# First feed-forward layer in two half-precision parts, with scales found on the chip, more planned time for the scales' round trips, and two more exponential buffers

## The chip, the cores and the metric

The kernel runs on one core of a Trainium2 chip. A core has five engines with a queue each: TensorE (PE in the profile; its weight loads are the row PEld) multiplies matrices into PSUM; VectorE (DVE), ScalarE (ACT) and GpSimd (POOL) do elementwise work; SyncE (SP) here only starts DMA transfers. Each engine takes its instructions in the order in which the program gives them and waits on semaphores for the others. The metric is the device time of one execution in microseconds (us). Three executions of the kernel before took 1029.51, 1033.57 and 1035.02 us, so the median is 1033.57 us.

## The reference

A hash-masked attention over 4 batches of 8 heads, 768 positions of 64 elements, followed by a feed-forward layer ("MoE" by its name, with one expert) over 3072 tokens of 512 elements and a hidden size of 2048:

```python
mask = q_bucket[:, :, :, None] == k_bucket[:, :, None, :]   # 6 sign bits of q @ proj, k @ proj
scores = np.where(mask, scale * np.matmul(q, k.transpose(0, 1, 3, 2)), -1000000000.0)
attn = np.exp(scores - np.max(scores, axis=-1, keepdims=True))
attn = attn / (np.sum(attn, axis=-1, keepdims=True) + 1e-09)
x = np.matmul(attn, v)            # then (batch, head, seq, dim) -> (batch*seq, head*dim)
h = x @ w_in                      # 512 -> 2048
r = np.maximum(h, 0.0)
out = (s * (r * r) + b) @ w_out   # 2048 -> 512
```

The inputs q, k, v and proj are float32. The two weight matrices arrive as float64 and are read as pairs of 32-bit words.

## The kernel before, in words

**Attention.** A visit is one (batch, head); there are 32, in order, and a visit has three slots of 256 queries, so 96 slots. A slot handles two tiles of 128 queries by 768 keys. For each tile PE makes the scores in two halves (lines 519 and 520), DVE takes the row maximum (line 524), ACT the exponential with its row sum (525), DVE four small operations for the inverse (531 to 534), and POOL normalizes (543). The exponentials live in a ring of buffers `eb`: `NE` = 3 of them, plus two that are laid over the buffer `pb` in the first eight visits.

The first eight visits (batch 0; `late(w)` is false) multiply in float32: PE transposes the tile (570), ACT or DVE copies it out of PSUM (the helper's line 199), and PE multiplies it with the values (577). From visit 8 on (`late`), the tile is split into two half-precision parts by ACT and DVE (547, 548), transposed by a DMA (549), and multiplied with values that were split in the same way (584). For that the values of a batch are scaled by a power of two that the chip finds. `value_scale` loads the eight heads' values one after another into `vm` (484), takes the largest absolute value of each (485, DVE), writes the 128 row maxima to DRAM (489), reads them back spread over all partitions (490), and DVE makes the scale out of them (494 to 499). Lines 489 and 490 are the *round trip*: both are issued by SP, and 490 waits until the write of 489 is done. It is made for batches 1, 2 and 3.

**Preparing a visit.** Transposes of q and k (384), their split in two parts (386, 387), the hash product (401 to 403), its mask bits (405) and several SP transfers that stack the operands (`ks`, `aq`, `bq`, all issued by the helper on line 175). A visit is prepared while the visit before it runs.

**Handing over to the feed-forward layer.** After its second head, a pair of heads' result (`xpb`, lines 603 and 604) is split into a high and a low part in fp32r, a rounded 32-bit format (`xsb`; ACT or POOL copy on 199, POOL subtraction on 609). SP writes the parts to DRAM (`xd`) and reads them back as `xc` (631).

**Weights.** 32 blocks of 128 by 512 float64 words are fetched on ACT's queue (338) and decoded to float32 by two ACT (340, 341), two DVE (342, 343) and one POOL instruction (344). A copy and a POOL subtraction (347) make the two fp32r parts. The order is four blocks of `w_in`, four of `w_out`, and so on.

**Feed-forward.** A chunk is 256 tokens; there are 12. A chunk has eight units of two blocks of 128 hidden elements. A unit multiplies in three passes per block of 128 (high weight by high input, low weight by high input, high weight by low input: lines 645, 646, 647; 24 matmuls of 256 columns), then takes the rectifier (651), the square (652), scale and bias (653, 654), the low part (655), and multiplies with `w_out` in three passes (666 to 668; 12 matmuls of 512 columns). The whole kernel has 2304 matmuls of the first kind.

**What sets the order.** Nothing runs as written. `Plan` collects every step with its engine, an estimated duration, what it reads and writes, a priority `pr` and a `lag` (time until its result is there). `order()` plays these on a model clock: whichever engine is free takes the ready step of the lowest priority number. A step may name several engines (`any`, `some`, `copy`), and goes to the one that is done first. The resulting order is each engine's program. Attention goes ahead of the units, which have priority numbers from 1e5 on and so fill what PE has left. The first units can run once slot 21 has been handed over.

Of the kernel before, what the change touches and what calls it, by code (L numbers as in the profile page):

```python
# [10 lines left out]
F32 = mybir.dt.float32  # L11
# [128 lines left out]
def lsh_attention_moe(ctx: ExitStack, tc, q, k, v, proj, w_in, w_out, s, b, out):  # L140
# [3 lines left out]
    P = 128  # L144
# [71 lines left out]
    vsc = tile_("vsc", [P, B, 2])  # L216
    VB = [tile_(f"vb{x}", [P, NT, 4, D], F16) for x in range(2)]
# [27 lines left out]
    xsb = tile_("xsb", [P, 2, CH], F32R)  # L245
# [67 lines left out]
    dec, wt = [], {}  # L313
# [7 lines left out]
    def decode(u, pr):  # L321
        src, key = dec[u]
        box = {}

        def new():
            box["t"] = wk.tile([P, 512, 2], I32, tag=f"w{u}", name=f"raw{u}")

        def swap():
            wt[key] = wk.tile([P, 2, 512], F32R, tag=f"w{u}", name=f"w{u}")
# [3 lines left out]
        rk, wk_ = [("raw", u)], [key + (0,), key + (1,)]  # L333
# [6 lines left out]
        act(512, lambda: nc.scalar.activation(g, raw()[:, :, 1].bitcast(F32), AF.Copy, scale=float(2.0**-112)), rk + [("pace", u % PACE)], [gk], pr)  # L340
        act(512, lambda: nc.scalar.activation(raw()[:, :, 0], raw()[:, :, 0].bitcast(U32), AF.Copy, scale=float(2.0**-29)), rk, rk, pr)
        dve(256, lambda: nc.vector.tensor_scalar(raw()[:, :, 1], gi, -2**31, None, ALU.bitwise_and), [gk], rk, pr, 0.54)
        dve(512, lambda: nc.vector.scalar_tensor_tensor(gi, gi, 3, raw()[:, :, 1], ALU.logical_shift_left, ALU.bitwise_or), rk, [gk], pr, 0.88)
        pool(512, lambda: nc.gpsimd.tensor_tensor(gi, gi, raw()[:, :, 0], ALU.add), rk, [gk], pr)
        plan.add(None, 0.0, swap, [], rk + wk_, pr)
        copy(512, lambda: wt[key][:, 0], lambda: g, [gk], [key + (0,)], pr, (ACT, POOL))
        pool(512, lambda: nc.gpsimd.tensor_tensor(wt[key][:, 1], g, f32(wt[key][:, 0]), ALU.subtract), [gk, key + (0,)], [key + (1,)], pr)  # L347
# [131 lines left out]
    def value_scale(bb, pr):  # L479


        for h in range(H):
            vd = v[bb, h].rearrange("(p t) d -> p t d", t=NT)
            plan.add(SP, 0.7, lambda vd=vd: nc.sync.dma_start(vm.rearrange("p (t d) -> p t d", t=NT), vd), [], ["vm"], pr, 196608 / RATE_DMA)
            dve(1, lambda h=h: nc.vector.tensor_reduce(vmx[:, h:h + 1], vm, AX.X, ALU.max, apply_absolute_value=True), ["vm"], [("vx", h)], pr, 0.5)
        m = vmx[:, H:H + 1]
        dve(1, lambda: nc.vector.tensor_reduce(m, vmx[:, 0:H], AX.X, ALU.max), [("vx", h) for h in range(H)], ["vx"], pr, 0.16)
        dm = tc.dram_tile([P], F32, name=f"vmax{bb}")
        plan.add(SP, 0.7, lambda: nc.sync.dma_start(dm.rearrange("(p o) -> p o", o=1), m), ["vx"], [("dm", bb)], pr, 0.3)
        plan.add(SP, 0.7, lambda: nc.sync.dma_start(vm[:, 0:P], dm.rearrange("(o x) -> o x", o=1).broadcast_to([P, P])), [("dm", bb)], ["vm"], pr, 0.3)  # L490
        up, down = vsc[:, bb, 0:1], vsc[:, bb, 1:2]

        def power():
# [3 lines left out]
            nc.vector.tensor_scalar(up.bitcast(I32), down.bitcast(I32), -1, 254 << 23, ALU.mult, ALU.add)  # L497
            nc.vector.tensor_scalar(up, up, float(2.0**14), None, ALU.mult)
            nc.vector.tensor_scalar(down, down, float(2.0**-14) * STEP / TOP, None, ALU.mult)
        dve(1, power, ["vm"], ["vx", ("sc", bb)], pr, 1.1)  # L500
# [54 lines left out]
    def values(i, pr, pieces):  # L555
# [45 lines left out]
        sa, sd = (vsc[0:D, bb, 1:2], vsc[D:P, bb, 1:2]) if late(w) else (1.0, 1.0)  # L601
        sk = [("sc", bb)] if late(w) else []
        some(CH, lambda e: e.activation(xh, av[0:D], AF.Copy, scale=sa) if e is nc.scalar else e.tensor_scalar(xh, av[0:D], sa, None, ALU.mult), [("b", 4)] + sk, xk, pr, (ACT, DVE))
        dve(CH, lambda: nc.vector.scalar_tensor_tensor(xh, av[D:P], sd, xh, ALU.mult, ALU.add), [("b", 4)] + sk, xk, pr, 0.42)
        if hh:

            xk = [tk + (0,), tk + (1,)]
            copy(CH, lambda: xsb[:, 0, :], lambda: t, xk, [("xs", 0)], pr, (ACT, POOL))
# [120 lines left out]
RATE = 6.0  # L729
PACE = 2  # L730
DSTART = 3
NNAT = 1
TOP = 2.0**27
STEP = 2.0**12
TWO = 2
# [39 lines left out]
```

## Time and profile before

| | us |
|---|---|
| median of three executions | 1033.57 |
| the profiled execution's own time | 1031.19 |
| its span, first to last instruction | 1029.4 |
| PE busy | 957.0 |
| DVE busy | 643.6 |
| ACT busy | 638.2 |
| POOL busy | 604.5 |

The profile is of one execution. Its own time is 2.4 us below the median, and 1.8 us lie outside the span. A row of a group of instructions gives line, engine, operation, operands, count, busy time and mean duration. A matmul's duration runs from its start to the end of its pipeline, and the next one starts before that end. So what a matmul costs PE is the distance between two starts, which the timeline shows.

### The profile page before, as it was taken

The page shows a single profiled execution, that of the slowest core. Times are in us where ns is not written, and L with a number is a line of the kernel's source. Part 1 is how long each engine was busy: PE and PEld are TensorE (multiplying, and loading weights), DVE is VectorE, ACT ScalarE, POOL GpSimd, SP SyncE. Part 2 cuts the span into 40 slices and gives each one's busy share as a digit, 9 for nine tenths or more (in the row PEclk, how much of TensorE's full clock was granted, in tenths as well). Part 3 has the DMA queues.
Part 4 walks back from the last instruction along what each step waited for, and adds up shares of the span by engine and source line. Part 5 has one row for each costly group of instructions (what it writes and reads, how often), then busy time and mean ns, then how long its engine had stood idle before and what let it go on. Part 6 is the DMA issues. An engine that isn't in the chain of part 4 may idle for free.

```text
span 1029.4 us, 17335 instructions
## 1 busy us (share of the span) xinstructions
PE 957.0 (93%) x6072; PEld 818.4 (80%) x6072; DVE 643.6 (63%) x1207; ACT 638.2 (62%) x1128; POOL 604.5 (59%) x559
## 2 busy tenths in 40 slices
PE   7977787698799999999999999999999999999998
PEld 5655555387678898888888998888888788999986
DVE  6786986688776667778877777777877661000000
ACT  2576777577666667767777667667776674334342
POOL 1356876599786657556656575756566555333333
PEclk6896999899899999999999999999999999999999
DMA  3276766587798798899899798899898773101000
GB/s 79 78 178 177 215 169 152 145 228 192 123 215 159 158 218 184 176 211 179 180 217 195 153 226 163 171 203 177 154 231 165 150 166 73 62 1 62 22 21 21
DMA packets 318791, 155.61 MB, mean 151 GB/s; under 512 B 283040, under 2 KB 291104, under 8 KB 318704
## 3 DMA queue, kind: packets, MB, share of 16 engines
q1 hardware_dynamic: 313504, 137.46, 62.2%
q10 hardware_dynamic: 5200, 17.05, 6.4%
q8 instruction: 48, 0.79, 0.3%
q14 instruction: 39, 0.32, 0.1%
HBM read 53.15 MB, written 18.88 MB: 70 GB/s over the span
## 4 chain that ended last, share of the span: by engine, by line
PE 53%; POOL 14%; issue 13%; DVE 10%; DMA 6%; ACT 3%; SPq 0%; POOLq 0%; DVEq 0%; ACTq 0%
PE bank L584 8%; PE bank L519 5%; PE bank L520 5%; PE bank L645 5%; PE bank L668 5%; PE bank L646 4%; POOL glb L655 4%; PE bank L666 4%; PE bank L647 4%; PE bank L667 4%; POOL rb L654 3%; POOL eb L543 2%; DVE st L524 2%; PE bank L577 2%; PE bank L570 2%
## 5 line engine op out<-in xcount | busy, mean ns | idle before, releaser
L543 POOL TENSOR_SCALAR eb<-eb,st 128x768 f32<-128x768 f32 x174 | 182.4, 1055 | 116.3 <-DVE st L534 99.6
L645 PE MATMUL bank<-xc,w 128*128 128x256 f32 x768 | 222.4, 290 | 5.3 <-DMA xc<-xd 2.7
L646 PE MATMUL bank<-xc,w 128*128 128x256 f32 x768 | 218.3, 284 | 3.6 <-POOL w L347 3.6
L647 PE MATMUL bank<-xc,w 128*128 128x256 f32 x768 | 217.7, 283 | 0.0
L524 DVE TENSOR_REDUCE st<-bank 128x1 f32<-128x768 f32 x192 | 180.8, 952 | 47.2 <-PE bank L520 36.9
L525 ACT ACTIVATE eb<-bank,st 128x768 f32<-128x768 f32 x174 | 155.9, 897 | 61.6 <-DVE st L524 30.7
L654 POOL TENSOR_SCALAR rb<-rb,misc 128x512 f32<-128x512 f32 x96 | 81.0, 843 | 174.4 <-ACT ghb L653 172.5
L548 DVE SCALAR_TENSOR_TENSOR pb<-pb,eb 128x768 f16<-128x768 f16 x144 | 157.9, 1106 | 36.4 <-ACT pb L547 33.5
L519 PE MATMUL bank<-ks,aq 128*128 128x384 f32 x384 | 143.4, 373 | 16.5 <-ACT eb L525 7.6
L547 ACT ACTIVATE pb<-eb 128x768 f16<-128x768 f32 x144 | 120.3, 839 | 60.6 <-POOL eb L543 41.0
L668 PE MATMUL bank<-w,glb 128*128 128x512 f32 x384 | 152.0, 396 | 5.1 <-POOL glb L655 5.0
L645 PEld LDWEIGHTS bank<-xc,w 128*128 128x128 f32 x768 | 147.1, 192 | 11.5 <-DMA xc<-xd 3.7
L666 PE MATMUL bank<-w,ghb 128*128 128x512 f32 x384 | 154.6, 403 | 0.0
L646 PEld LDWEIGHTS bank<-xc,w 128*128 128x128 f32 x768 | 147.4, 192 | 7.1 <-POOL w L347 3.9
L667 PE MATMUL bank<-w,ghb 128*128 128x512 f32 x384 | 152.5, 397 | 0.0
L647 PEld LDWEIGHTS bank<-xc,w 128*128 128x128 f32 x768 | 147.2, 192 | 0.0
L655 POOL TENSOR_TENSOR glb<-rb,ghb 128x512 fp32r<-128x512 f32 x96 | 136.2, 1419 | 5.8
L520 PE MATMUL bank<-ks,bq 76*128 76x384 f32 x384 | 135.3, 352 | 3.3 <-DMA bq<-nat 3.3
L651 ACT ACTIVATE rb<-bank 128x512 f32<-128x512 f32 x72 | 42.9, 596 | 128.6 <-PE bank L647 126.0
L584 PE MATMUL bank<-tb,vb 128*128 128x256 f16 x864 | 108.1, 275 | 1.3 <-DMA tb<-pb 0.7
L519 PEld LDWEIGHTS bank<-ks,aq 128*128 128x128 f32 x384 | 76.1, 198 | 36.1 <-ACT eb L525 11.7
L679 DVE COPY osb<-bank 128x256 f32<-128x256 f32 x4 | 1.5, 420 | 160.4 <-PE bank L668 159.7
(111 smaller groups left out, 1615.8 us busy)
## 6 DMA issues: line engine op xcount, KB each, us to landing
xd<-xsb SPq DMA_DIRECT2D x48, 256.0 KB
xc<-xd SPq DMA_DIRECT2D x48, 256.0 KB
ks<-aq SPq DMA_DIRECT2D x60, 192.0 KB
raw<-in_moe_w_in_dram ACTq DMA_DIRECT2D x16, 512.0 KB
raw<-in_moe_w_out_dram ACTq DMA_DIRECT2D x16, 512.0 KB
nat<-in_q_dram SPq DMA_DIRECT2D x32, 192.0 KB
nat<-in_k_dram SPq DMA_DIRECT2D x32, 192.0 KB
ks<-bq SPq DMA_DIRECT2D x30, 192.0 KB
```

Source lines behind the costliest of these rows:

```text
L519: nc.tensor.matmul(o, aq[:, ts], ks[0][:, cols], start=True, stop=False)
L520: nc.tensor.matmul(o, bq[0:HR, ts], ks[1][0:HR, cols], start=False, stop=True)
L524: dve(S, lambda a=a, sc=sc: nc.vector.tensor_reduce(nm[:, a:a + 1], sc, AX.XY, ALU.max, negate=True), bk, [nk[a]], pr, 0.95)
L543: eng.tensor_scalar(e, e, rz[:, a:a + 1], u[:, a:a + 1], ALU.mult, ALU.add)
L584: nc.tensor.matmul(av, VB[x][:, kt, 2 * h:2 * h + 2].rearrange("p z d -> p (z d)"), t[:, :, h, kt], start=(h == kt == 0), stop=(h == 1 and ...
L645: nc.tensor.matmul(hp, w[:, 0, fs], xc[:, 0, :], start=(cc == 0), stop=False)
L646: nc.tensor.matmul(hp, w[:, 1, fs], xc[:, 0, :], start=False, stop=False)
L647: nc.tensor.matmul(hp, w[:, 0, fs], xc[:, 1, :], start=False, stop=(cc == NC_ - 1))
L655: pool(2 * CH, lambda r=r, gh=gh, gl=gl: nc.gpsimd.tensor_tensor(gl, r, f32(gh), ALU.subtract), [rk, hk], [lk], MP)
L666: nc.tensor.matmul(o, gh[:, ts], w[:, 0], start=(f == 0), stop=False)
L667: nc.tensor.matmul(o, gh[:, ts], w[:, 1], start=False, stop=False)
L668: nc.tensor.matmul(o, gl[:, ts], w[:, 0], start=False, stop=(f == NF - 1))
```

## The change

It has four pieces.

1. **First layer in half precision.** `w_in` and the handed-over result become two float16 parts instead of two fp32r parts (`xsb`, `xd`, `xc`, `wt` of the `wi` blocks). The number of matmuls, their columns and their passes stay. The planner's duration for three of them becomes 0.327 us, where it was 0.358 us.
2. **Scales found on the chip.** A float16 part needs its input scaled by a power of two. There is a scale per batch for the values, now also for batch 0, and one for each group of four `wi` blocks. For a `wi` block DVE takes a maximum of 512 elements. After the fourth block of a group the maxima go on a round trip as above (`spread`), DVE makes the scale (`power`), and the four blocks, which have stayed in a ring of `NWR` = 6 raw buffers, are split: high part on ACT or POOL, low part on DVE in one instruction or on POOL in two. The rectifier multiplies by the product of the two scales (`dsc`). The first batch's hand-over makes its low part on DVE instead of POOL. In later batches the scaling of `xpb` is by a constant and no longer by the values' scale.
3. **Room for the round trips.** `spread` adds a step without an engine and with a lag of `SLACK` = 6 us after the write and another after the read. `value_scale` of the next batch starts with priority number +60 instead of +40, and its maxima may also be taken by ACT.
4. **Buffers.** `NE` goes from 3 to 5: five exponential buffers in the late visits, seven in the first eight.

```diff
-    NXP, NXC, NE = 3, 3, 3
+    NXP, NXC, NE = 3, 3, 5
-    xsb = tile_("xsb", [P, 2, CH], F32R)
+    xsb = tile_("xsb", [P, 2, CH], F16)
...
+        if wi:
+            n, j = key[1:]
+            dve(1, lambda: nc.vector.tensor_reduce(wmx[:, j:j + 1], raw()[:, :, 1].bitcast(F32), AX.X, ALU.max, apply_absolute_value=True), rk, [("wx", j)], pr, 0.65)
...
-        pool(512, lambda: nc.gpsimd.tensor_tensor(wt[key][:, 1], g, f32(wt[key][:, 0]), ALU.subtract), [gk, key + (0,)], [key + (1,)], pr)
...
+        spread(f"wmax{n}", m, "wx", wbc, "wbc", pr)
+        up, down = wsc[:, n, 0:1], wsc[:, n, 1:2]
...
+                some(512, lambda e: e.activation(wt[key_][:, 0], src_(), AF.Copy, scale=up) if e is nc.scalar else e.tensor_scalar(wt[key_][:, 0], src_(), up, None, ALU.mult), rk_ + [("wsc", n)], [key_ + (0,)], pr, (ACT, POOL))
...
+                plan.any([(DVE, 0.75, lambda: nc.vector.scalar_tensor_tensor(wt[key_][:, 1], src_(), up, wt[key_][:, 0], ALU.mult, ALU.subtract)),
+                          (POOL, 1.95, rest)], [("wsc", n), key_ + (0,)], rk_ + [key_ + (1,)], pr)
...
+    def spread(name, m, mk_, dst, dk, pr):
...
+        plan.add(SP, 0.7, lambda: nc.sync.dma_start(dm.rearrange("(p o) -> p o", o=1), m), [mk_], [name], pr, 0.3)
+        plan.add(None, 0.0, lambda: None, [], [name], pr, SLACK)
+        plan.add(SP, 0.7, lambda: nc.sync.dma_start(dst, dm.rearrange("(o x) -> o x", o=1).broadcast_to([P, P])), [name], [dk], pr, 0.3)
+        plan.add(None, 0.0, lambda: None, [], [dk], pr, SLACK)
...
-                    pe(mmc(CH, 3), mm, [boxes[cc][2], ("wi", f0 // 4, cc, 0), ("wi", f0 // 4, cc, 1)], [("b", 5)], fill)
+                    pe(0.327, mm, [boxes[cc][2], ("wi", f0 // 4, cc, 0), ("wi", f0 // 4, cc, 1)], [("b", 5)], fill)
...
+    value_scale(0, VZERO)
...
-        if c == h == 0 and (w + H < len(visits) or not bb) and any(late((bb + 1) * H + x) for x in range(H)) and bb + 1 < B:
-            value_scale(bb + 1, pr + 40)
+        if c == h == 0 and bb + 1 < B:
+            value_scale(bb + 1, pr + VLATE)
...
+NWR = 6
+SLACK = 6.0
+VLATE = 60
+VZERO = 10
```

More of the change, by code (lines that the diff above doesn't have):

```diff
@@ L323, in decode @@
         box = {}
+        wi, kin = key[0] == "wi", u // (NC_ + 4) * NC_ + key[-1]
+        tag = f"wr{kin % NWR}" if wi else f"w{u}"
         def new():
[L326 to L329 removed]
+            box["t"] = wk.tile([P, 512, 2], I32, tag=tag, name=f"raw{u}")
         def raw():
             return box["t"]
[L333 removed]
+        rk, wk_ = [("raw", tag)], [key + (0,), key + (1,)]
         g, gk = osb[:, u % 2, :], ("os", u % 2)
@@ L345, in decode, with swap @@
-        plan.add(None, 0.0, swap, [], rk + wk_, pr)
-        copy(512, lambda: wt[key][:, 0], lambda: g, [gk], [key + (0,)], pr, (ACT, POOL))
-        pool(512, lambda: nc.gpsimd.tensor_tensor(wt[key][:, 1], g, f32(wt[key][:, 0]), ALU.subtract), [gk, key + (0,)], [key + (1,)], pr)
+        if not wi:
+            def swap():
+                wt[key] = wk.tile([P, 2, 512], F32R, tag=f"w{u}", name=f"w{u}")
+            pool(512, lambda: nc.gpsimd.tensor_tensor(gi, gi, raw()[:, :, 0], ALU.add), rk, [gk], pr)
+            plan.add(None, 0.0, swap, [], rk + wk_, pr)
+            copy(512, lambda: wt[key][:, 0], lambda: g, [gk], [key + (0,)], pr, (ACT, POOL))
+            pool(512, lambda: nc.gpsimd.tensor_tensor(wt[key][:, 1], g, f32(wt[key][:, 0]), ALU.subtract), [gk, key + (0,)], [key + (1,)], pr)
+            return
@@ new lines, in decode, with power @@
+        pool(512, lambda: nc.gpsimd.tensor_tensor(raw()[:, :, 0], gi, raw()[:, :, 0], ALU.add), [gk], rk, pr)
+        held_raw.append((raw, rk, key))
+        if j < NC_ - 1:
+            return
+        m = wmx[:, NC_:NC_ + 1]
+        dve(1, lambda: nc.vector.tensor_reduce(m, wmx[:, 0:NC_], AX.X, ALU.max), [("wx", x) for x in range(NC_)], ["wx"], pr, 0.16)
+        spread(f"wmax{n}", m, "wx", wbc, "wbc", pr)
+        up, down = wsc[:, n, 0:1], wsc[:, n, 1:2]
+        def power():
+            di = down.bitcast(I32)
+            nc.vector.tensor_reduce(m, wbc, AX.X, ALU.max)
+            nc.vector.tensor_scalar(di, m.bitcast(I32), 0x7FF00000, None, ALU.bitwise_and)
+            nc.vector.tensor_scalar(di, di, 8, -(896 << 23), ALU.mult, ALU.add)
+            nc.vector.tensor_scalar(down, down, float(2.0**-100), None, ALU.max)
+            inverse_power(up, down)
@@ L600, in values @@
         xh, xk = t[hh * D:(hh + 1) * D], [tk + (hh,)]
[L601 to L604, printed above, removed]
+        scale = STEP / TOP if late(w) else 1.0
@@ L605, in values @@
+        some(CH, lambda e: e.mul(xh, av[0:D], scale) if e is nc.scalar else e.tensor_scalar(xh, av[0:D], scale, None, ALU.mult), [("b", 4)], xk, pr, (ACT, DVE))
+        dve(CH, lambda: nc.vector.scalar_tensor_tensor(xh, av[D:P], scale, xh, ALU.mult, ALU.add), [("b", 4)], xk, pr, 0.42)
         if hh:
             xk = [tk + (0,), tk + (1,)]
-            copy(CH, lambda: xsb[:, 0, :], lambda: t, xk, [("xs", 0)], pr, (ACT, POOL))
-            pool(CH, lambda: nc.gpsimd.tensor_tensor(xsb[:, 1, :], t, f32(xsb[:, 0, :]), ALU.subtract), xk + [("xs", 0)], [("xs", 1)], pr)
@@ L610, in values @@
-            xd[key] = tc.dram_tile([P, 2, CH], F32R, name=f"xd{key[0]}_{key[1]}_{key[2]}")
-            dma(lambda: xd[key], lambda: xsb, [("xs", 0), ("xs", 1)], [("xd", key)], pr, 262144)
+            if late(w) != late(w - 1):
+                raise ValueError("both heads of a pair in one way")
+            up = vsc[:, bb, 0:1]
+            if late(w):
+                copy(CH, lambda: xsb[:, 0, :], lambda: t, xk, [("xs", 0)], pr, (ACT, POOL))
+                pool(CH, lambda: nc.gpsimd.tensor_tensor(xsb[:, 1, :], t, xsb[:, 0, :], ALU.subtract), xk + [("xs", 0)], [("xs", 1)], pr)
+            else:
+                some(CH, lambda e: e.activation(xsb[:, 0, :], t, AF.Copy, scale=up) if e is nc.scalar else e.tensor_scalar(xsb[:, 0, :], t, up, None, ALU.mult), xk + [("sc", bb)], [("xs", 0)], pr, (ACT, POOL))
+                dve(CH, lambda: nc.vector.scalar_tensor_tensor(xsb[:, 1, :], t, up, xsb[:, 0, :], ALU.mult, ALU.subtract), xk + [("sc", bb), ("xs", 0)], [("xs", 1)], pr, 0.45)
```

55 lines of the change are left out of this document (40 added, 15 removed).

## The prediction

> **What bounds the kernel now.** I read the busy time by stages first, then the timeline of PE, then the chain of waits and the queues of SP and DVE where that chain leaves the engines.
>
> The stages (length, busy time and count of each engine, granted clock, DMA share, GB/s):
>
> ```profile
> 0.00:200.00 200.00, 156.99 (x892) 109.73 (x892) 147.12 (x336) 117.36 (x234) 109.46 (x116) 0.87 0.60 151
> 200.00:310.00 110.00, 94.77 (x564) 79.86 (x562) 90.15 (x143) 78.96 (x138) 97.18 (x75) 0.94 0.82 185
> 310.00:835.00 525.00, 515.74 (x3413) 459.02 (x3413) 393.03 (x703) 363.53 (x637) 323.91 (x296) 1.00 0.89 183
> 835.00:1029.00 194.00, 189.55 (x1209) 169.77 (x1208) 13.33 (x26) 78.40 (x120) 73.95 (x74) 1.00 0.17 47
> ```
>
> The columns are PE, PEld, DVE, ACT, POOL. From 310 us on PE is busy 98% at full clock, so there the time is the sum of PE's steps, and faster elementwise work brings nothing. Before 200 us PE has only attention, is busy 78% and loses clock; nothing else is full either, so that stage runs at the pace of the attention's chains. From 200 to 310 POOL is the fullest (97.2 of 110 us), since the last weights are decoded there beside the first units. The whole is thus a start whose length is set by chains, and a packed rest. A microsecond saved on PE counts in the rest, and one saved on the chains counts in the start; PE fills up after it whatever the start took.
>
> **PE's steps.** Durations of matmuls overlap, so I take distances between starts:
>
> ```profile
> 902.42 0.28 PE L645 MATMUL bank<-xc,w 128*128 128x256 f32 x1
> ...
> 905.28 0.39 PE L666 MATMUL bank<-w,ghb 128*128 128x512 f32 x1
> ```
> ```profile
> 404.88 0.40 PE L668 MATMUL bank<-w,glb 128*128 128x512 f32 x1
> 405.12 1.48 PE L584 MATMUL bank<-tb,vb 128*128 128x256 f16 x12
> 406.36 0.48 PE L666 MATMUL bank<-w,ghb 128*128 128x512 f32 x1
> 406.68 0.40 PE L667 MATMUL bank<-w,ghb 128*128 128x512 f32 x1
> ```
>
> One unit's 24 fp32r matmuls (two blocks of three passes over four slices of the input) run from 902.42 to 905.28: 2.86 us, 119.2 ns each. Twelve half-precision matmuls of the same tile and columns, with the change of format before and after them, take from 405.12 to 406.68 less one step of 512 columns (0.24, as from 404.88 to 405.12): 1.32 us, 110.0 ns each. The difference is 9.2 ns. The Trainium skill speaks against this saving: its page "TensorE: Matmul & The Clock Gate", section "Back-to-back issue gap", has columns over 2.4 GHz plus 2.5 ns, 109 ns for 256 columns, and makes no difference by type. The half-precision row agrees with it, the fp32r row at 119.2 doesn't; by it the sum would lose this term.
>
> How many matmuls lie where PE is the bound, by the third of them that has line 645:
>
> ```profile
> 310.00:835.00 525.00, 123.98 (x428) 81.12 (x428) 1.00 0.89 183
> 835.00:1029.00 194.00, 71.55 (x253) 48.12 (x253) 1.00 0.17 47
> ```
>
> After 310 us 3 x 681 = 2043, times 9.2 ns, is 18.8 us. The other 261 of 2304 give 2.4 us, of which I count half, as POOL and not PE is fullest there. **Term 1: -20 us.** Its ends: where units are cut by attention the runs are shorter than twelve and pay the change of format more often. If all of the 0.08 us by which the step at 406.36 is longer than usual were such a price and the rest 0.103 us each, runs of eight would cost 113 ns, and the term would be -13 us. If runs were as long as a unit with the same price, 24 would cost 107 ns, and it would be -28 us.
>
> **The round trips.** The chain of waits in the start (start, length, what):
>
> ```profile
> 66.72 11.18 DMA xd<-xsb
> 78.32 5.97 DMA bq<-nat
> ...
> 167.92 7.91 DMA vmax<-vmx
> 177.14 6.21 DMA ks<-aq
> ```
>
> Both long pieces lie where a scale makes its trip (the first is put down to a transfer in the same queue). The queue of SP and DVE's waits show why:
>
> ```profile
> 72.66 0.49 SPq L175 DMA_DIRECT2D aq<-aq  x1
> 77.18 0.32 SPq L490 DMA_DIRECT2D vm<-vmax  x1
> ```
> ```profile
> 167.92 0.58 SPq L489 DMA_DIRECT2D vmax<-vmx  x1
> 176.12 0.33 SPq L490 DMA_DIRECT2D vm<-vmax  x1
> 176.53 1.20 SPq L175 DMA_DIRECT2D ks<-aq  x2
> ```
> ```profile
> 182.39 0.29 DVE L494 TENSOR_REDUCE vmx<-vm 128x1 f32<-128x128 f32 x1 [7.04 <-DMA vm<-vmax]
> ```
>
> SP stands at line 490 until the write has landed, 4.0 us the first time (73.15 to 77.18) and 7.6 us the second (168.50 to 176.12); behind it stand operands of the next visit (`bq`, issued at 78.32 by the chain, and `ks`), for which PE waits. Then DVE stands at line 494, 7.04 us the second time, with all row maxima behind it. From 167.92 to 182.39 the trip takes 14.5 us. The planner of before allows for 0.7 + 0.3 + 1.8 us twice, 5.6 us, and so puts both instructions too early in their queues. What that costs is read from visits, which have six row maxima (line 524) each:
>
> ```profile
> 57.00:85.70 28.70, 5.70 (x6) 0.87 0.81 187
> 85.70:106.70 21.00, 5.74 (x6) 0.77 0.59 160
> 106.70:126.80 20.10, 5.64 (x6) 1.00 0.76 215
> 126.80:145.70 18.90, 5.46 (x6) 1.00 0.66 172
> 145.70:167.30 21.60, 5.74 (x6) 1.00 0.62 183
> 167.30:200.70 33.40, 5.70 (x6) 0.85 0.68 140
> ```
>
> The four visits in between take 20.4 us on average, the two with a trip 8.3 and 13.0 us more: 21 us. The third trip falls among the units:
>
> ```profile
> 267.25 0.87 SPq L489 DMA_DIRECT2D vmax<-vmx  x1
> 278.72 0.33 SPq L490 DMA_DIRECT2D vm<-vmax  x1
> ```
> ```profile
> 286.05 0.39 PE L645 MATMUL bank<-xc,w 128*128 128x256 f32 x1 [2.11 <-DMA xc<-xd]
> ```
>
> SP stands 10.6 us (268.12 to 278.72), but PE has units, and the trip shows as the 2.11 us for which it waits for inputs that SP issued late: 3 us with what follows. With twice 6 us of lag the planner allows for 17.6 us, more than the 14.5 us of the trip and, on its first leg, 8.8 us against waits of 4.0, 7.6 and 10.6 us. So SP still stands up to 2 us at a trip, and DVE hardly at all. **Term 2: -24 us** before what the change adds; ends 0 and -24.
>
> **What it adds to the start.** There are five trips more: batch 0's values and four groups of weights. With the lags I take each at nothing, as SP's 1 or 2 us lie beside work that doesn't wait for it, and at 8 us (a third of term 2) if the lags don't help. DVE gets work, priced by these rows (the first three give minimum, median and maximum):
>
> ```profile
> L485 DVE TENSOR_REDUCE vmx<-vm x24: 533/543/554, 23.7 to 253.8; 128x1 f32<-128x384 f32 x24
> L343 DVE SCALAR_TENSOR_TENSOR osb<-osb,raw x32: 676/886/1778, 65.8 to 292.1; 128x512 int32<-128x512 int32 x32
> L347 POOL TENSOR_TENSOR w<-osb,w x32: 1262/1282/2049, 70.6 to 298.5; 128x512 fp32r<-128x512 f32 x32
> L199 DVE COPY tb<-bank 128x512 f32<-128x512 f32 x21 | 14.1, 685 | 4.5 <-PE bank L570 4.4
> 0.00:200.00 200.00, 22.34 (x17) 0.87 0.60 151
> ```
>
> The last row counts line 347: 17 of 32 blocks are decoded before 200 us, 9 of them of `w_in`. Each costs DVE a maximum (543 ns for 384 elements, 0.72 for 512) and a low part (0.89 by line 343): 9 x 1.61 = 14.5 us. Batch 0's values: 8 x 0.54 = 4.3. The hand-over's low part, 12 x 0.45 (half of line 343) = 5.4. Three scales at about 1 us: 3. Together 27 us, while POOL loses 9 x 1.28 = 12 us and the hand-over's subtractions. How full DVE is in undisturbed visits:
>
> ```profile
> 110.00:135.00 25.00, 19.75 (x122) 13.09 (x120) 22.21 (x46) 17.91 (x37) 19.18 (x20) 1.00 0.70 193
> 135.00:160.00 25.00, 21.43 (x144) 15.51 (x144) 21.23 (x47) 19.31 (x39) 17.27 (x19) 1.00 0.66 177
> ```
>
> 87%, so there is little room, and what isn't moved away lengthens the stage. The planner can move 14.1 us of `tb` copies to ACT, and the value maxima of two batches (8.6 us, partly). I let 17 of the 27 us go and 10 us stay: at 87% that is 11 us. The ends are 0 (all is moved) and 31 us (nothing is). The seven exponential buffers may shorten the chains a little; no row shows a wait for such a buffer, so I take 0. **Term 3: +11 us.**
>
> The Trainium skill, page "SBUF — State Buffer", section "Who interferes with whom", says that a DVE instruction with two SBUF inputs blocks against a GpSimd instruction that reads SBUF, for its whole length. Line 343's spread, 676 to 1778 ns, agrees. By the rule the low parts, which have two such inputs, would cost up to 1.78 instead of 0.89 us, and the sum would be that of rival three.
>
> **From 200 to 310.** POOL loses 7 x 1.28 = 9 us of 97; DVE, at 90 of 110 us, gains 7 x 1.61 + 3 = 14 us. One fullest engine replaces the other: 0, ends -8 and +8. The last group of weights now needs a trip before its first unit, 14.5 us behind its decode, beside the `w_out` blocks: +3, ends 0 and +14. After 310 us the smaller `xd` and `xc` transfers and the deeper ring lie under PE: 0. **Term 4: +3 us.**
>
> **The sum.** -20 - 24 + 11 + 3 = -30 us. The profiled execution took 1031.19 us and would take 1001.2; it lies 2.4 us below the median, so against the median 1033.57 the forecast is 1004 us, by its own terms between 994 and 1014 (0.48).
>
> **Rivals.** *One: the start gains in full.* The planner finds room on ACT and POOL for all of DVE's new work, and POOL's relief of 8 us from 200 to 310 is half kept: -20 - 24 - 4, or 986 us. For it speaks that ACT is busy only 117 of the first 200 us, against it that the low parts of the weights can't go there. 0.20. *Two: the trips are only covered.* Behind them something else comes just as late, such as the operands' own transfers (`bq` took 5.97 us on the chain): terms 2 to 4 cancel, term 1 stays, 1014 us. 0.15. *Three: DVE becomes the bound.* Nothing is moved or the low parts block against POOL: +31 instead of +11, and +8 from 200 to 310: 1032 us, no change. 0.06. *Four: the format brings nothing,* because short runs eat it: term 1 gone, 1024 us. 0.04. The gap of the Trainium skill's page on TensorE, above, would give the same. *Five: slower.* The lag lives on the planner's clock; on the chip a queue comes to the read as early as before, and all eight trips hold SP and DVE for the 8 us that the three did: 64 us come in for the 24, and the sum is -20 - 24 + 64 + 14 = +34, or 1068 us. It decides from (20 + 24 - 14) / 8 = 3.8 us per trip. Against it: the lag of 12 us is nearly the length of the trip. 0.07.
>
> **How the numbers follow.** A measurement of this kernel can tell about 0.5% from no change, 1028 to 1039 us. The forecast and rivals one, two and four end below that, with 0.87 in all; some of the edge of four lies inside, so faster 0.86, same 0.07, slower 0.07. The range 978 to 1026 takes in these four with term 1's and term 3's ends, and leaves out three and five.
>
> **What would show it.** Right: 24 matmuls of lines 645 to 647 in about 2.6 us; no DVE wait over 2 us at a scale's reduction; visits in the first 200 us that all take 20 to 23 us; DVE over 90% there; PE at 98% from before 300 us on. Wrong: a step of 119 ns in half precision (rival four), SP or DVE standing over 4 us at most trips (five), slots after 200 us that start no earlier than before (two or three, which DVE's share tells apart), or PE waiting for the last group's weights by more than 5 us.

## The result and the profile after

The kernel after takes 1044.4 us (median of 4 executions, 1039.86 to 1046.28), the kernel before on the same chip 1033.08 us (4 executions). The ratio is 1.0107, with a 95% interval from 1.0064 to 1.0150: slower by 11 us, where 30 us less were forecast. The profiled execution took 1039.86 us and has a span of 1038.1 us (before: 1029.4).

The stages of the kernel after, in the columns that the prediction explains:

```profile
0.00:200.00 200.00, 155.17 (x855) 108.36 (x856) 152.18 (x356) 125.39 (x259) 103.64 (x100) 0.87 0.54 143
200.00:310.00 110.00, 78.83 (x462) 59.80 (x461) 84.47 (x159) 69.65 (x126) 80.91 (x63) 0.84 0.73 144
310.00:835.00 525.00, 511.91 (x3457) 420.46 (x3456) 397.10 (x725) 373.43 (x669) 327.93 (x293) 1.00 0.88 174
835.00:1038.00 203.00, 196.93 (x1306) 160.70 (x1303) 20.96 (x38) 89.26 (x135) 81.80 (x80) 1.00 0.19 44
```

From 200 to 310 us every engine is now *less* busy than before: PE 78.8 us against 94.8, POOL 80.9 against 97.2, DVE 84.5 against 90.2. No engine became the bound. They all wait for something.

Since PE catches up later, the best measure of the start is how many matmuls PE has behind it at a fixed time. The same view with one cut, at 400 us, and PE alone, first of before, then of after (length, PE's busy time and count, granted clock, DMA share, GB/s):

```profile
0.00:400.00 400.00, 339.02 (x2024) 0.92 0.72 166
400.00:1070.00 670.00, 618.03 (x4050) 1.00 0.63 133
```
```profile
0.00:400.00 400.00, 317.00 (x1851) 0.89 0.67 151
400.00:1070.00 670.00, 625.85 (x4223) 1.00 0.63 126
```

Both programs have 6074 recorded matmuls. At 400 us the kernel after is 173 behind. From there on before needs 629.4 us for 4050, or 155.4 ns each, and after 638.1 us for 4223, or 151.1 ns. So the start loses 173 x 155.4 ns = 26.9 us, and the rest gains 4223 x 4.3 ns = 18.2 us; together +8.7 us, the difference of the two spans. The split takes all matmuls alike, though their kinds differ in columns. Most of the loss is idle time of PE (83.0 us of the 400, where it was 61.0). With it go a lower granted clock and a longer busy time per matmul (171.3 ns at 0.89, 167.5 at 0.92).

**The part that came as forecast.** The 24 matmuls of a unit at the end of the kernel after:

```profile
910.16 0.28 PE L708 MATMUL bank<-xc,wi 128*128 128x256 f16 x1
...
912.69 0.27 PE L710 MATMUL bank<-xc,wi 128*128 128x256 f16 x1
912.72 0.48 PE L733 MATMUL bank<-w,ghb 128*128 128x512 f32 x1
913.03 0.40 PE L734 MATMUL bank<-w,ghb 128*128 128x512 f32 x1
```

2.56 us, where it was 2.86. The step of 512 columns behind them takes 0.31 instead of 0.24 us; with these 0.07 us the 24 cost 110 ns each. The change of format shows no price of its own: from the start of the last half-precision matmul (912.69) to that of the second one of 512 columns (913.03) it is 0.34 us, which is one step of each kind (0.11 and 0.24).

**The part that did not.** The visits of the start in the kernel after, each with its six row maxima on DVE (now line 581):

```profile
54.90:78.50 23.60, 5.70 (x6) 0.93 0.63 187
78.50:108.30 29.80, 5.73 (x6) 0.83 0.59 151
108.30:135.00 26.70, 5.62 (x6) 0.81 0.60 161
135.00:156.00 21.00, 5.65 (x6) 0.84 0.50 132
156.00:183.50 27.50, 5.72 (x6) 0.94 0.58 163
183.50:211.80 28.30, 5.70 (x6) 0.94 0.71 194
```

No visit but one is near 20.4 us. What the queue of SP waits for at the round trips (lines 398, the write, and 400, the read; us in all, times, longest):

```profile
SPq L398 <- DVE wmx L364: 13.7, 3, 7.8
SPq L398 <- DVE vmx L548: 5.9, 3, 4.7
SPq L400 <- DMA wmax<-wmx: 4.6, 2, 4.0
SPq L400 <- DMA vmax<-vmx: 3.4, 1, 3.4
```

In the kernel before (lines 489 and 490):

```profile
SPq L490 <- DMA vmax<-vmx: 22.1, 3, 10.5
...
SPq L489 <- DVE st L524: 0.5, 1, 0.5
...
SPq L489 <- DVE osb L343: 0.4, 1, 0.4
```

The wait for the write to land, 22.1 us in three trips of the kernel before, has shrunk to 8.0 us in eight, as planned. But SP now stands for 19.6 us one instruction earlier, at the write, since the maximum that it is to write isn't there; before it stood there for 0.9 us. Behind it stand other transfers, such as the loads of q and k for a later visit. DVE has no wait at a scale's reduction.

Of the weights' four trips, which take 23.2, 27.5, 24.5 and 35.3 us from maximum to scale, that of the last group is the longest. Queue of SP, then DVE and PE:

```profile
256.51 0.35 SPq L398 DMA_DIRECT2D wmax<-wmx  x1
...
261.74 8.16 SPq L606 DMA_TRANSPOSE tb<-pb  x1
...
271.87 0.66 SPq L400 DMA_DIRECT2D wbc<-wmax  x1
```
```profile
256.34 0.14 DVE L364 TENSOR_REDUCE wmx<-wmx 128x1 f32<-128x4 f32 x1
...
280.34 0.16 DVE L588 TENSOR_SCALAR bank<-st 128x2 f32<-128x2 f32 x1 [11.80 <-PE bank L641]
...
291.60 0.28 DVE L370 TENSOR_REDUCE wmx<-wbc 128x1 f32<-128x128 f32 x1
```
```profile
277.49 2.74 PE L641 MATMUL bank<-tb,vb 128*128 128x256 f16 x12 [9.89 <-DMA tb<-pb]
...
293.67 0.40 PE L708 MATMUL bank<-xc,wi 128*128 128x256 f16 x1 [3.42 <-ACT wi L384]
...
295.90 0.40 PE L709 MATMUL bank<-xc,wi 128*128 128x256 f16 x1 [1.84 <-DVE wi L389]
```

From maximum to scale it takes 35 us, where the planner allows 17.6. The three trips of before took 15.7, 14.5 and 16.7 us from the write to the reduction; the last of them was:

```profile
267.25 0.87 SPq L489 DMA_DIRECT2D vmax<-vmx  x1
```
```profile
283.94 0.29 DVE L494 TENSOR_REDUCE vmx<-vm 128x1 f32<-128x128 f32 x1
```

In the kernel after, SP issues the last group's read 15 us after the write, with a transpose of line 606 in between that holds its queue for 8.16 us. DVE comes to the reduction 20 us after the read, since it has itself stood 11.80 us for PE. PE has stood 9.89 us because the transposes of attention came late, with no unit placed there to fill the gap, and then waits 3.42 + 1.84 us for the weights themselves. Up to 310 us it runs 7 units (counted by line 720), the kernel before 10.

### The profile page after: what moved, and what is told of

Read it like the earlier page. It is cut to its first block, busy times and chain, and to the rows that moved or that the text cites. A ratio compares the mean times of both kernels' runs of the same rounds, so it can differ in the third digit from the quotient of the medians.

```text
span 1038.1 us, 17440 instructions
## 1 busy us (share of the span) xinstructions
PE 942.8 (91%) x6072; PEld 749.3 (72%) x6072; DVE 654.7 (63%) x1275; ACT 657.7 (63%) x1186; POOL 594.3 (57%) x535
## 4 chain that ended last, share of the span: by engine, by line
PE 48%; issue 14%; POOL 12%; DVE 10%; DMA 10%; ACT 4%; SPq 1%; POOLq 0%; DVEq 0%; ACTq 0%
PE bank L641 7%; PE bank L576 5%; PE bank L577 4%; POOL glb L722 4%; PE bank L708 4%; PE bank L735 4%; DMA tb<-pb 4%; PE bank L709 4%; PE bank L710 4%; PE bank L733 4%; PE bank L734 4%; POOL rb L721 3%; DMA nat<-in_k_dram 2%; POOL eb L600 2%; PE bank L634 2%
## 5 line engine op out<-in xcount | busy, mean ns | idle before, releaser
L600 POOL TENSOR_SCALAR eb<-eb,st 128x768 f32<-128x768 f32 x179 | 210.1, 1181 | 155.1 <-DVE st L591 134.1
L708 PE MATMUL bank<-xc,wi 128*128 128x256 f16 x768 | 212.0, 276 | 3.4 <-ACT wi L384 3.4
L709 PE MATMUL bank<-xc,wi 128*128 128x256 f16 x768 | 210.0, 273 | 1.8 <-DVE wi L389 1.8
L710 PE MATMUL bank<-xc,wi 128*128 128x256 f16 x768 | 210.1, 274 | 0.0
L582 ACT ACTIVATE eb<-bank,st 128x768 f32<-128x768 f32 x179 | 160.1, 895 | 59.2 <-DVE st L581 56.5
L721 POOL TENSOR_SCALAR rb<-rb,misc 128x512 f32<-128x512 f32 x96 | 83.9, 874 | 168.8 <-ACT ghb L720 168.8
L576 PE MATMUL bank<-ks,aq 128*128 128x384 f32 x384 | 151.3, 394 | 29.1 <-ACT eb L582 18.2
L733 PE MATMUL bank<-w,ghb 128*128 128x512 f32 x384 | 160.5, 418 | 0.0
L734 PE MATMUL bank<-w,ghb 128*128 128x512 f32 x384 | 152.5, 397 | 0.0
L604 ACT ACTIVATE pb<-eb 128x768 f16<-128x768 f32 x144 | 119.8, 836 | 32.2 <-DMA tb<-pb 19.3
L718 ACT ACTIVATE rb<-bank,dsc 128x512 f32<-128x512 f32 x72 | 49.4, 687 | 119.3 <-PE bank L710 110.8
L708 PEld LDWEIGHTS <-wi 128*128 128x128 f16 x768 | 75.2, 98 | 47.0 <-issue 36.0
L641 PEld LDWEIGHTS <-vb 128*128 128x128 f16 x864 | 82.7, 99 | 31.1 <-DMA tb<-pb 11.9
L735 PEld LDWEIGHTS bank<-w,glb 128*128 128x128 f32 x384 | 72.6, 189 | 26.6 <-POOL glb L722 9.1
```

Of the source, the lines that this page charges most:

```text
L576: nc.tensor.matmul(o, aq[:, ts], ks[0][:, cols], start=True, stop=False)
L600: eng.tensor_scalar(e, e, rz[:, a:a + 1], u[:, a:a + 1], ALU.mult, ALU.add)
L641: nc.tensor.matmul(av, VB[x][:, kt, 2 * h:2 * h + 2].rearrange("p z d -> p (z d)"), t[:, :, h, kt], start=(h == kt == 0), stop=(h == 1 and ...
L708: nc.tensor.matmul(hp, w[:, 0, fs], xc[:, 0, :], start=(cc == 0), stop=False)
L709: nc.tensor.matmul(hp, w[:, 1, fs], xc[:, 0, :], start=False, stop=False)
L710: nc.tensor.matmul(hp, w[:, 0, fs], xc[:, 1, :], start=False, stop=(cc == NC_ - 1))
```

## The experiments

Eighteen kernels. Every ratio is to the kernel before on the same chip, and where two experiments are compared, their ratios are subtracted and taken times 1033 us. In the expectations the theories have letters, in short: A, finding scales lengthens the start; B, the order that the planner happens on; C, the deeper ring of exponentials; D, the units' wait for the last group's scale; E, the load of the maxima and trips themselves, whoever waits for them. The columns: median in us, ratio with its interval, matmuls done at 400 us in the profiled execution, and ns per matmul from there to the end of the span.

| kernel | us | ratio | at 400 us | ns after |
|---|---|---|---|---|
| before | 1033.08 | 1 | 2024 | 155.4 |
| after | 1044.40 | 1.0107 [1.0064, 1.0150] | 1851 | 151.1 |
| format_only | 1015.57 | 0.9848 [0.9817, 0.9879] | 1993 | 150.1 |
| format_room | 1013.39 | 0.9825 [0.9779, 0.9871] | 1983 | 150.4 |
| room_only | 1020.34 | 0.9914 [0.9887, 0.9942] | 2113 | 156.5 |
| no_room | 1062.55 | 1.0302 [1.0266, 1.0337] | 1758 | 152.7 |
| both_fixed | 1023.66 | 0.9953 [0.9924, 0.9982] | 1926 | 151.6 |
| w_fixed | 1023.19 | 0.9918 [0.9885, 0.9951] | 1956 | 151.1 |
| v_fixed | 1047.83 | 1.0177 [1.0157, 1.0198] | 1832 | 152.3 |
| ne3 | 1042.99 | 1.0121 [1.0074, 1.0167] | 1826 | 150.3 |
| format_ne5 | 1021.92 | 0.9913 [0.9889, 0.9938] | 1992 | 151.8 |
| prio50 | 1040.48 | 1.0080 [1.0049, 1.0111] | 1861 | 151.7 |
| trips_unused | 1032.70 | 1.0019 [0.9985, 1.0052] | 1922 | 154.2 |
| last_fixed | 1024.86 | 0.9949 [0.9926, 0.9971] | 1976 | 153.3 |
| last_unused | 1034.20 | 1.0032 [1.0004, 1.0061] | 1917 | 153.4 |
| w_in_first | 1041.85 | 1.0098 [1.0067, 1.0128] | 1825 | 150.9 |
| pe_spread | 1026.92 | 0.9937 [0.9908, 0.9966] | 1978 | 152.1 |
| pe_spread_ne3 | 1028.11 | 0.9953 [0.9921, 0.9985] | 1969 | 151.9 |
| pe_v_fixed | 1028.87 | 0.9972 [0.9954, 0.9989] | 1952 | 151.3 |
| pe_w_fixed | 1006.21 | 0.9766 [0.9717, 0.9816] | 2054 | 150.0 |

Among the kernels in half precision the last column goes from 150.0 to 154.2 ns, which is worth up to 17 us over some 4150 matmuls. The column before it goes from 1758 to 2054 matmuls, worth 45 us, and tells more. Both are of one execution. Where that one lies well above the median (trips_unused by 9 us, both_fixed by 7, last_unused and last_fixed by 5), they show the kernel too slow.

### Which piece costs what

**both_fixed, w_fixed, v_fixed.** Constants take the place of the found scales of the weights (2^14), of batch 0's values (2^12) or of both; maxima and trips go with them, and a `w_in` block is split as soon as it is decoded.

```diff
+    nc.vector.memset(vsc[:, 0, 0:1], float(2.0**12))
+    nc.vector.memset(vsc[:, 0, 1:2], float(2.0**-12))
...
+    nc.vector.memset(wsc[:, :, 0], float(2.0**14))
+    nc.vector.memset(wsc[:, :, 1], float(2.0**-14))
...
-            dve(1, lambda: nc.vector.tensor_reduce(wmx[:, j:j + 1], raw()[:, :, 1].bitcast(F32), AX.X, ALU.max, apply_absolute_value=True), rk, [("wx", j)], pr, 0.65)
...
-        spread(f"wmax{n}", m, "wx", wbc, "wbc", pr)
...
-        dve(1, power, ["wbc"], ["wx", ("wsc", n)], pr, 1.1)
...
-    value_scale(0, VZERO)
```

> Leaves out finding a scale for the weights and for batch 0's values: both are fixed powers of two (2^14 and 2^12); the rest is the changed kernel (half precision, room, five buffers). Theory A, the start is lengthened by the work of finding scales (DVE's maxima, eight loads of values, five more trips): visit 8 starts at 195 us or sooner (212 in the changed kernel) and the time falls to about 1015 us. Theory B, the start is lengthened by the order itself, which the planner chose on a clock that the chip doesn't follow: visit 8 stays at 205 us or later and the time stays above 1030 us.

> Leaves out only finding the weights' scale (fixed 2^14; each block is split at once, no maxima, no trips, no held blocks). Theory A: a part of the gain of the run with both fixed, and if the held blocks and the trips of the weights are the cost, most of it: 1020 to 1025 us, and units 5 to 8 of the first chunk without the gap from 267 to 305 us. If batch 0's values are the cost: 1038 us or more. Theory B: 1030 to 1045 us, no pattern.

> Leaves out only finding the scale of batch 0's values (fixed 2^12: no eight loads in the first 110 us, no trip). Theory A with the values' loads as the cost (they stand in SP's queue beside the loads of q and k, whose wait is the largest DMA piece of the chain): visit 4 starts at 95 us instead of 108 and the time is about 1030 us. With the weights as the cost: 1040 us. Theory B: anything from 1030 to 1050 us.

Neither theory came out whole: the time of both_fixed falls, as A has it, but not to 1015 us, and visit 8 is late, as B has it. w_fixed meets A's 1020 to 1025 us; v_fixed speaks against the values' loads as the cost: visit 4 starts at 103.3 us and not at 95, and the time does not fall.

Finding the weights' scales costs 0.9918 to 1.0107, or +19.5 us, by one pair and 0.9953 to 1.0177, or +23 us, by the other. Finding the scale of batch 0's values costs nothing that shows: without it the kernel isn't faster in either pair, and v_fixed is even slower than after by 7 us, with intervals that do not touch. That is also a warning: each edit makes the planner write another order, and taking work away can cost 7 us. Differences below that are not given a mechanism here. both_fixed begins visit 8 at 217.8 us, later than after's 211.8, so in this trace the visits are long without these scales, too.

**format_only, format_room, room_only, no_room.** Half precision with both scales fixed, three buffers and the old planning; the same with the room; the room alone in the kernel before; and the kernel after with the room taken out.

```diff
-    NXP, NXC, NE = 3, 3, 5
+    NXP, NXC, NE = 3, 3, 3
...
-SLACK = 6.0
-VLATE = 60
+SLACK = 0.0
+VLATE = 40
```
```diff
+        plan.add(None, 0.0, lambda: None, [], [("dm", bb)], pr, SLACK)
...
+        plan.add(None, 0.0, lambda: None, [], ["vm"], pr, SLACK)
...
-            value_scale(bb + 1, pr + 40)
+            value_scale(bb + 1, pr + 60)
```

> Half precision alone: both scales fixed, three buffers, lags of 0, priority +40; it leaves out finding the weights' and batch 0's scale. Term 1 of the prediction alone: 20 us below the kernel before, 1010 to 1013 us, with visit 8 at 200 us as before. Theory C says the same. Theory B: 1010 to 1035 us, with visit 8 later than 205 us in the worse half.

> Half precision with both scales fixed, three buffers and the room of 6 us (lags, priority +60); it leaves out finding the weights' and batch 0's scale. If the gain of the room (9.5 us on the kernel before) and that of the format (18 us) add up: 1005 us. If the 8 us by which the kernel with both scales fixed is behind the format alone come from the room: 1023 us; if they come from the five buffers: 1005 us, too.

> The kernel before with nothing changed but the lags of 6 us after both legs of the three round trips and the priority of the next batch's scale (+60). If term 2 of the prediction holds, the two long visits (28.7 and 33.4 us) shrink to about 20 to 22 us, visit 8 starts at about 182 us and the time is 1010 to 1015 us. If the trips only covered other waits: 1030 to 1035 us.

> The changed kernel with lags of 0 and the priority +40 as before: eight trips with no room. If the room is worth what the three trips cost before (8 us a trip in the start): 1060 to 1080 us, with DVE waits of several us at the scales' reductions. If the room brings nothing: 1040 to 1048 us. Theory B: scatter between 1030 and 1055 us.

The format, with the small moves of work that come with it (the hand-over's low part on DVE, the constant in `xpb`), brings 15.7 us (12.5 to 18.9 by the interval). Its visit 8 starts at 206.4 us, not at the 200 expected. The room brings 9 us in the kernel before (6 to 12), 2 us beside the fixed scales (the intervals overlap) and 20 us in the kernel after, which has eight trips for three. So format_room misses the 1005 us at which the two gains would add up, room_only its 1010 to 1015 us and the short visits, and no_room lies in its expected range. Without it the trips show as the old ones did, at the read and at DVE:

```profile
SPq L400 <- DMA wmax<-wmx: 15.0, 3, 7.4
SPq L400 <- DMA vmax<-vmx: 12.8, 3, 5.9
```
```profile
DVE vmx L553 <- DMA vm<-vmax: 7.3, 2, 6.2
```

In room_only the waits at the read are gone, and SP stands 2.2, 2.1 and 1.0 us at the write. Yet the visits do not come down to 20.4 us. The two trips of the start leave SP at 67.0 and 160.6 us, with their reads at 82.7 and 174.1; the two visits that hold them take 26.5 and 28.2 us, and the one behind the second 25.8:

```profile
56.00:82.50 26.50, 5.70 (x6) 0.94 0.64 177
...
145.80:174.00 28.20, 5.55 (x6) 0.89 0.84 180
174.00:199.80 25.80, 5.71 (x6) 0.92 0.72 194
```
```profile
0.00:400.00 400.00, 346.42 (x2113) 0.95 0.74 172
```

Visit 8 starts at 199.8 us, where it was 200.8. The gain of room_only comes behind that: 89 matmuls ahead at 400 us, and 12 units up to 310 us instead of 10.

**ne3, format_ne5, prio50.** The ring of exponentials at 3 in the kernel after; at 5 in format_only; and the kernel after with another priority for the later batches' values, which changes little but the order.

```diff
-    NXP, NXC, NE = 3, 3, 5
+    NXP, NXC, NE = 3, 3, 3
```
```diff
-VLATE = 60
+VLATE = 50
```

> The changed kernel with three exponential buffers instead of five (five instead of seven in the first eight visits). Theory C, the deeper ring is what lengthens the start, as it lets scores and exponentials run ahead of the work that frees the operands of the next visit: visit 8 starts at 200 us or sooner (212 in the changed kernel) and the time falls to 1015 to 1025 us. Theory B, the order's luck: 1030 to 1050 us with visit 8 anywhere. Theory A, already weakened by the run with both scales fixed (visit 8 at 218 us): 1044 us, no change.

> Half precision with both scales fixed and five buffers, without the room (lags 0, priority +40); it leaves out finding the weights' and batch 0's scale. If the buffers cost 10 us: 1025 us, against 1016 us with three. If the 10 us were the order's luck: anything between 1010 and 1025 us, and no later visits than with three.

> A probe of the order's luck: the changed kernel with the next batch's scale at priority +50 instead of +60, and nothing else. Theories A and C: within 5 us of the changed kernel's 1044 us. Theory B: it moves by 8 us or more, though the work is the same.

Theory C falls: ne3 is no faster. Two more buffers cost 13 us from format_room to both_fixed and 6.7 us from format_only to format_ne5, and bring 1.4 us from ne3 to after and 1.7 us from pe_spread_ne3 to pe_spread (both inside the intervals). They do no good that can be measured, and do harm only where the weights' scales are fixed. What the harm is stays open. It also means that pairs at five buffers show the weights' scales too cheap: at three buffers, from format_room (0.9825) to ne3 (1.0121), finding all scales costs 30.6 us. prio50 differs from after by 2.8 us, inside the intervals, where theory B wanted 8 or more.

### What of the weights' scales costs

**trips_unused, last_fixed, last_unused, w_in_first.** All maxima and trips of the weights are made, but blocks are split at once with 2^14; the last of the four groups alone gets the constant and no maxima; the last group's maxima and trip are made, but its split uses the constant at once; all 16 `w_in` blocks are decoded ahead of the `w_out` blocks, so that the last group's scale is there early.

```diff
+    wsf = tile_("wsf", [P, NG, 2])
+    nc.vector.memset(wsc[:, :, 0], float(2.0**14))
+    nc.vector.memset(wsc[:, :, 1], float(2.0**-14))
...
-        if j < NC_ - 1:
-            return
...
-        dve(1, power, ["wbc"], ["wx", ("wsc", n)], pr, 1.1)
+        if j == NC_ - 1:
+            dve(1, power, ["wbc"], ["wx", ("wsf", n)], pr, 1.1)
```
```diff
+            fixed = n == NG - 1
+            if not fixed:
+                dve(1, lambda: nc.vector.tensor_reduce(wmx[:, j:j + 1], raw()[:, :, 1].bitcast(F32), AX.X, ALU.max, apply_absolute_value=True), rk, [("wx", j)], pr, 0.65)
...
-        if j < NC_ - 1:
+        if j < NC_ - 1 and not fixed:
```
```diff
+        free = n == NG - 1
+        if j < NC_ - 1 and not free:
...
+            dve(1, power, ["wbc"], ["wx", ("wsf",) if free else ("wsc", n)], pr, 1.1)
```
```diff
+    for f0 in range(0, DF, 512):
...
-            while nd[0] < f0 // 4 * 8 + 6 + f0 % 4:
+            while nd[0] < DF // 512 * NC_ + f0 + 2:
```

> The weights' maxima, their four trips and the scales' arithmetic stay, but their result is not used: every block is split at once with a fixed 2^14. Theory D, the units' wait for a scale is what the 21 us between the changed kernel and the one with fixed weights' scales consist of: about 1023 us, and the gap before the seventh unit is 35 us or less. Theory E, it is the load of the maxima and trips on DVE and SP: about 1040 us, however the split is timed.

> The changed kernel with a fixed scale for the last of the four groups only; it leaves out that group's maxima and trip. Theory D: nearly the whole 21 us come back, 1025 us, since only the last group's trip has a unit waiting behind it. Theory E: a quarter of them, 1038 us.

> The changed kernel, in which the last group's maxima and trip are made but its four blocks are split at once with a fixed 2^14. If the wait for the trip's result is the cost: like the run with the last group fixed, 1025 us. If the trip itself and the maxima are, by their places in SP's and DVE's queues: like the changed kernel, 1040 us or more.

> The changed kernel with all sixteen w_in blocks decoded ahead of the w_out blocks, so that the last group's trip lies before the first unit. Theory D: the gap before the seventh unit shrinks to 20 us or less and the time is about 1025 us. Theory E: 1044 us, as the same work is on DVE and SP.

last_fixed is 16 us faster than after (0.9949 against 1.0107, intervals apart): of the 19.5 us that the weights' scales cost, nearly all belong to one group of four, as theory D had it. (By the 30.6 us at three buffers it would be about half.) Its profile has 125 matmuls more done at 400 us, 29 of them already at 250 us, ahead of that group's trip:

```profile
0.00:400.00 400.00, 331.17 (x1976) 0.91 0.70 156
```

last_unused lies between, 7.7 us under after and 8.6 us over last_fixed, and trips_unused likewise, 9 us under after and 10 us over w_fixed. So D and E each seem to be about half; since both steps are near the 7 us that another order can make, the split isn't settled. w_in_first, at 0.9 us under after, decides nothing: the gap of the last `w_in` group is gone, but the `w_out` blocks are now the late ones, and PE waits 8.4 us for them between 200 and 330 us.

### The trip itself

**pe_spread and its three versions.** All eight trips through DRAM are replaced. DVE multiplies the identity with the row maxima, PE multiplies that with ones, which puts all 128 maxima on every partition of a corner of PSUM that is not used otherwise, and DVE takes the maximum there. All scales are still found. pe_spread_ne3 has three buffers, and from it pe_v_fixed and pe_w_fixed fix batch 0's values or the weights' scale, as above.

```diff
-        plan.add(SP, 0.7, lambda: nc.sync.dma_start(dm.rearrange("(p o) -> p o", o=1), m), [mk_], [name], pr, 0.3)
-        plan.add(None, 0.0, lambda: None, [], [name], pr, SLACK)
-        plan.add(SP, 0.7, lambda: nc.sync.dma_start(dst, dm.rearrange("(o x) -> o x", o=1).broadcast_to([P, P])), [name], [dk], pr, 0.3)
-        plan.add(None, 0.0, lambda: None, [], [dk], pr, SLACK)
...
+        o = bank[:, 0, HS:HS + P]
+        dve(P, lambda: nc.vector.tensor_scalar(wbc, ident, m, None, ALU.mult), [mk_], ["wbc"], pr, 0.25)
+        pe(0.25, lambda: nc.tensor.matmul(o, ones, wbc, start=True, stop=True), ["wbc"], ["sp"], pr)
```

> The changed kernel without any trip through DRAM: DVE multiplies the identity by the row maxima, PE multiplies an all-ones matrix with that, and DVE takes the maximum from PSUM, for the weights and the values alike. All maxima, loads and dependences stay. If the trips cost what the runs so far say (21 us for the weights', a few for the values'): 1015 to 1025 us. If the maxima and loads are the cost: 1035 to 1044 us.

> The same with three exponential buffers. If the five buffers cost 10 us as they did with fixed scales: 1005 to 1015 us, below every kernel so far. If that was the order's luck: within 5 us of the run with five, on either side.

> As the run with three buffers and the maxima spread by PE (1028 us), with a fixed 2^12 for batch 0's values; it leaves out their eight loads and maxima. If the values are the remaining 12 us: 1016 us. If the weights are: 1026 to 1030 us. Order's luck: up to 8 us off either.

> The same kernel with a fixed 2^14 for w_in instead; it leaves out the weights' maxima and splits each block at once. If the weights are the remaining 12 us: 1016 us. If the values are: 1026 to 1030 us. Order's luck: up to 8 us off either.

The last group's way from maximum to scale in pe_spread, on DVE:

```profile
274.56 0.15 DVE L366 TENSOR_REDUCE wmx<-wmx 128x1 f32<-128x4 f32 x1
...
277.36 0.28 DVE L372 TENSOR_REDUCE wmx<-bank 128x1 f32<-128x128 f32 x1
```

2.8 us for the 35 of after. Five of the eight take 2.2 to 3.3 us like this one; the other three take 9.4, 17.8 and 37.7 us, since their steps lie far apart in the queues. pe_spread is 17.6 us faster than after (intervals apart, and 2 us short of what was expected) and, with every scale found on the chip, beats the kernel before by 0.6% (0.3 to 0.9). PE at 400 us, first in pe_spread, then in pe_w_fixed:

```profile
0.00:400.00 400.00, 335.90 (x1978) 0.89 0.65 156
```
```profile
0.00:400.00 400.00, 343.38 (x2054) 0.91 0.68 163
```

Fixing batch 0's values changes nothing here either (+2.0 us, inside the intervals). Fixing the weights' scale brings 19.3 us, and pe_w_fixed, which finds no scale of the weights, is the fastest of all at 1006.2 us. At three buffers, then, the weights' scales cost 19 us when PE spreads them and some 30 us by way of DRAM. So about a third of their price is the trip. The rest must lie in the maxima and in the wait of a block, which could be split when it is decoded, for its three neighbours; no run separates these two. pe_w_fixed is 10 us below the 1016 expected. The three trips of the values are worth 6 us (format_room, 0.9825, to pe_w_fixed; the intervals overlap).

## Why the prediction was wrong

**Term 1 (-20) was right, inside its ends of -13 and -28.** The rest of the kernel gains 18.2 us, and format_only 15.7 as a whole. The Trainium skill's page "TensorE: Matmul & The Clock Gate", section "Back-to-back issue gap", has for isolated matmuls the columns over 2.4 GHz plus 2.5 ns, by which 256 columns of any type would take an estimated 109 ns. The half-precision step agrees, 110 ns; the 119.2 ns of fp32r in the kernel before do not, and rival four, which that rule would have given, fell.

**Term 2 (-24) failed in size.** Alone, in the kernel before, the room brings 9 us, and hardly any of it in the visits. The step that failed took the excess of "the two with a trip 8.3 and 13.0 us more: 21 us" for the price of the stall. The visits without a trip were to be what the others would become, but without the stall at the read three visits still take 26.5, 28.2 and 25.8 us. Something else in them is as late, as rival two had it for the whole. What it is, no experiment isolated.

**"With the lags I take each at nothing" failed.** Eight trips were worth 17.6 us in all (after to pe_spread), 2.2 us each; without the room they are worth 37.7 us (no_room to pe_spread, which keeps the later priority), 4.7 us each. The prediction missed two things. The lag removes most of SP's wait at the read and does nothing for the wait at the write, where SP stands for DVE's maximum. Nor does it hold off what the planner lays between write and read, such as the 8.16 us transpose: the weights' trips, allowed 17.6 us, take 23 to 35. Which of the two makes the price isn't shown. SP's wait at the write can't be the whole of it: in ne3 it is 5.8 us where after has 19.6, SP never waits for a write to land, and the time is the same. The price per trip is rival five's mechanism, but with the room it stays below the 3.8 us at which that rival decides; the last group's wait came on top, and the room brought less.

**Term 3 (+11) looked in the wrong place.** DVE gets its new work and is busy 152.2 of the first 200 us, 76% (74% before), not over 90%. The scale of batch 0's values costs nothing in three pairs. So the visits aren't long for want of DVE; that they are for want of operands is argued, not shown.

**Term 4 (+3) is the term that was mis-sized.** Its sentence was "The last group of weights now needs a trip before its first unit, 14.5 us behind its decode, beside the `w_out` blocks: +3, ends 0 and +14". The group costs 16 us (after to last_fixed), above the upper end. The prediction took the trip at 14.5 us, the shortest of the three of before, and it was 35. And +3 for a trip of 14.5 us takes most of the wait as covered by other units, which were not there: after has one wait of 9.89 us for the transposes of attention with no unit left to fill it. prio50 has it too (10.1 us between 200 and 330 us), ne3 in three pieces (9.0 us), and last_fixed and w_fixed have no wait there. But trips_unused, whose units wait for no scale, has 6.9 us of it, so the missing units are not the whole cause. PE's waits for the weights themselves are no part of the price: they are 5.3 us in after, and 6.7 us in last_fixed and 8.0 us in w_fixed. That the last group is the cause of the 16 us is shown, up to the 7 us that another order can make; by which way it is, is not.

**The buffers (0)** brought 1.4 us from ne3 to after; that they cost 13 and 6.7 us elsewhere stays open.

By one path through the experiments at three buffers the sum is: format -15.7, room -2.4, finding the scales +30.6, the two buffers -1.4, together +11.1 us. Against the forecast's terms (-20, -24, +11 and +3 for what the scales add, 0) the misses are 4, 22, 17 and -1 us, which make up the 41 us between -30 and +11. By this path, which has the prediction's order, about half of the miss is the room that brought too little, and most of the other half the scales, above all the last group's. The pieces don't add up independently of the order, though. With the room put in last the sum is: format -15.7, the two buffers +6.7, finding the scales +40.2 (format_ne5 to no_room), room -20.1. Then the room is nearly the -24 forecast, and the scales with their trips miss by 26 us. Either way the scales cost two to three times the 14 us that terms 3 and 4 gave them, and the room is worth more the more trips there are.

## What to carry to other kernels

A wait in a planned queue that is given more planned time may move to the instruction ahead of it, and the planned time may be filled with other work: look at what the queue stands at and how long the whole trip takes, not only whether the old wait is gone. A value that all partitions need was better spread inside the core here (17.6 us for eight) than by a trip whose two DMA instructions share a queue with the operands of the critical stage. Where one engine fills up later whatever the start took, compare its count of finished instructions at a fixed time and its pace from there: the two numbers split a change into its start and its rest, as long as the mix of instructions stays alike. Pieces of a change that meet in one queue have no price of their own: measure each from both ends, in the kernel before and out of the kernel after.

## What the runs showed of the hardware

The issue of a DMA transpose, 1.5 us as a rule, can hold SP's queue for over 8 us. All 144 of the kernel after (ns, least, median and most):

```profile
L606 SPq DMA_TRANSPOSE tb<-pb x144: 1274/1518/8164, 232.1 to 867.7; - x144
```

The longest of the kernel before was 2.8 us. And the half-precision weight load is half as long, 98 ns as against 190, though the step from matmul to matmul fell only from 119 to 110 ns. After, then before:

```profile
L708 PEld LDWEIGHTS <-wi x768: 95/98/152, 188.2 to 1026.5; 128*128 128x128 f16 x192
```
```profile
L645 PEld LDWEIGHTS bank<-xc,w x768: 186/190/337, 170.2 to 1018.0; 128*128 128x128 f32 x192
```
